# A fused attention and two-MLP kernel: two column tiles per PSUM bank, wider vector steps and finer weight loads behind the attention

## The chip, the cores and the metric

The kernel runs on one core of a Trainium2 chip. The metric is the device time of one execution in microseconds. Three executions of the kernel before took 1026.25, 1027.25 and 1030.13 us; their median is 1027.25 us. PE is the matrix engine (its weight loads are shown apart, as PEld), DVE the vector engine, ACT the scalar engine, POOL GpSimd; SP issues the DMAs.

## The reference

Block-causal attention over 4 batches, 8 heads, 576 positions of 64 elements, then two MLPs on the 2304 x 512 result. Weights arrive as float64, everything is computed to float32 accuracy.

```python
scores = scale * np.matmul(q, k.transpose(0, 1, 3, 2))
scores = np.where(block_i >= block_j, scores, -1e9)      # blocks of 64 positions
attn = softmax(scores); x = (attn @ v) -> (2304, 512)
h = x @ w1_in;  x = (h * np.cos(h)) @ w1_out             # 512 -> 2048 -> 512
h = x @ w2_in;  r = np.maximum(h, 0); out = (r * r) @ w2_out
```

## The kernel before

Every float32 operand of the MLPs is split into a high and a low part (`hi_part`, `lo_part`), and each product is three matmuls (`mm3`): high by high, high by low, low by high. Weights are read as raw 8-byte words and rebuilt as float32 (`weight_piece`), then split.

**Order.** The program is first recorded as a list of operations; `schedule` then plans them with a cost for each, as a list scheduler would: it keeps a clock for each engine and for the DMA queue, and takes the ready operation with the lowest priority number. A priority is the place in the program plus a shift by kind and phase (`PUT_OFF`). Steps that several engines can do (`flexible`: the high part on POOL or ACT, the low part on DVE or POOL, copies on ACT or DVE) go where the planned end is earliest, with each engine's cost weighted by `BIAS` of the phase. The planned order is what each engine's queue gets. Phases: 0 and 1 are the attention, 2 is stage 0, 3 is stages 1 and 2.

**Attention and the first half of MLP 1.** The attention is interleaved with the products of the first 1024 of 2048 columns of MLP 1 (`first_in`, `first_out`), whose partial result goes to DRAM (`y1_d`). In the same stretch the weights of the later stages are prepared: `left_weights` builds linear combinations of the quarters of a weight chunk (`left_parts`), splits them and stores them to DRAM (`wi_d`) by way of two buffers `so`; `staged_weights` does the like for second-product weights (`wo_d`).

**Three stages behind the attention.** Stage 0 is the second half of MLP 1 (x from `x_d`, the result to `y_d`), stages 1 and 2 are the halves of MLP 2. Each takes the 2304 tokens in four chunks of 512 and one of 256. A chunk's first product is a fast product of 2 x 2 blocks with seven multiplications: `load_quarters` loads x, forms four differences (`add`) and splits seven operands; `quad` runs the seven products for one column tile of 128 in three PSUM banks `a`, `b`, `c` of which it uses 256 columns each, with the seven weight factors as stationary operands. Between the products, finished sums are copied out (`kept`: tiles `p1`, `u2`, `p5`) or added (`summed`), and handed to `sink`, which applies the nonlinearity (`turned`: h cos h in stage 0; `squared` in stages 1 and 2) and splits the result into `g`. Each chunk has two weight chunks `c` and in each two column tiles `m`, so four calls of `quad`. The last, short chunk goes through `two`, with plain products. Then comes the second product (`out_T` in stage 0, the loop over 128-token tiles in the others), 24 matmuls for each result bank.

**Weights of the first products.** A stage's factors are loaded from `wi_d` by `factors`: for each of the two weight chunks four tiles of 1 MB, each with two factors (high and low, both halves of K). The pool `wo` has four such places, `wa` eight, four of which hold the second-product weights `w2o`. The loads for the next stage are recorded at the end of a stage (stage 0: at the last chunk), and wait for the places.

**PSUM.** Eight banks are handed out by the planner (`Banks`): up to six for `h`, up to three for `y`, and behind the attention two are kept for `y`. A bank is one unit to the planner: a step that reads any of it follows all earlier matmuls into it.

Of the kernel before, what the change touches and what calls it, by code (L numbers as in the profile page):

```python
# [24 lines left out]
BIAS = [{"DVE": 1.01, "ACT": 0.29, "POOL": 0.23}, {"DVE": 3.3, "ACT": -0.66, "POOL": -0.23}, {"DVE": 0.9, "ACT": -2.27, "POOL": -0.09}, {"DVE": -0.14, "ACT": -1.34, "POOL": 0.87}]  # L25
# [14 lines left out]
PUT_OFF = [{"load": 2, "weights": -24, "prep": 6, "scores": 25, "weighted": 31, "split": 249, "in": -31, "cos": -170, "out": -11, "warm": 9160, "later": 931}, {"load": 494, "weights": -159, "prep": -70, "scores": 69, "weighted": -175, "split": 91, "in": -32, "cos": -169, "out": -21, "later": 855}, {"load": 283, "weights": 654, "prep": -58, "scores": 43, "weighted": -284, "split": 332, "in": -36, "cos": -49, "out": -46, "later": 600}, {"in": 2, "out": 132, "later": 93}]  # L40
# [322 lines left out]
def kernel(  # L363
# [252 lines left out]
    wi_d = [[T(dram, [128, 4, 512], F32, f"wi_d{c}{i}") for i in range(4)] for c in range(6)]  # L616
    wo_d = [[T(dram, [128, 4, 512], F32, f"wo_d{c}{i}") for i in range(2)] for c in range(2)]
# [122 lines left out]
    def left_parts(w, k, slots, stage):  # L740
# [9 lines left out]
        for i, x in enumerate((a11, a12, s4, a22, s1, s2, s3, a21)):  # L750
            to = slots[i // 2][:, i % 2 * 2:i % 2 * 2 + 2, cs]
            st = T(st_p, [128, 2, 256], F32R, "so", 2) if stage else to
            hi_part(st[:, 0], x)
            lo_part(st[:, 1], x, st[:, 0])
            if stage:
                dma(to, f(st), 262144)

    @of("later")
    def left_weights(w, c, slots, stage=False):

        gate = R.ops[-1:]
        for k in range(2):
            left_parts([weight_piece(w[i * 128:i * 128 + 128, c * 512:c * 512 + 512], gate) for i in (k, k + 2)], k, slots, stage)

    def slots_of(pool, n=8, k=4):
        return [T(pool, [128, 4, 512], F32R, "w", n) for _ in range(k)]

    @of("later")
    def staged_weights(srcs, to):

        gate = R.ops[-1:]
        for src, (hi_d, lo_d) in zip(srcs, to):
            for i in range(4):
# [3 lines left out]
                dma(hi_d[:, i], f(hi), 262144)  # L777
                lo_part(lo, w, hi)
                dma(lo_d[:, i], f(lo), 262144)

    def from_dram(pool, staged, n=8):

        got = slots_of(pool, n, len(staged))
        for t, s in zip(got, staged):
            dma(f(t), s, 1048576)
        return got

    def weights(pool, srcs, n=8):

        got = []  # L790
        for src in srcs:
            hi = T(pool, [128, 4, 512], F32R, "w", n)
            lo = T(pool, [128, 4, 512], F32R, "w", n)
            for i in range(4):
                weight_part(src[i * 128:(i + 1) * 128, :], hi[:, i], lo[:, i])
# [22 lines left out]
    def h_tile(w_in, m, xs, n):  # L818
# [3 lines left out]
        for kk in range(KD):  # L822
            mm3(
                ps[:, :n], (hi[:, kk, c], lo[:, kk, c]), (xs[0][:, kk], xs[1][:, kk]),
# [20 lines left out]
    def out_T(w_out, g, n, sink):  # L845

        for d in range(KD):
            ps = bank("y")[:, :n]
            for m in range(HALF):
# [3 lines left out]
                    ps, (hi[:, m % 4, c], lo[:, m % 4, c]), (g[0][:, m, :n], g[1][:, m, :n]), m == 0, m == HALF - 1  # L853
# [307 lines left out]
    for group, steps in WORK:  # L1161
# [6 lines left out]
        if group in ((0, 2), (1, 1)):  # L1168
            c = group[0]
            left_weights(w1_in, 2 + c, wi_d[c], True)  # L1170
# [6 lines left out]
        if group == (3, 2):  # L1177
            (tmp3,) = later(("tmp3",))
            transition(s1.close, ctx, [tmp3], (xs_p, tmp))
            left = factors(wi_d[:2])  # L1180
# [4 lines left out]
    def load_plain(src, c0, n):  # L1185

        ops = [[T(x3_p, [128, 2, 256], F32R, f"x{j}{i}") for j in "hl"] for i in range(2)]
        for i in range(KD):
            t = T(x3_p, [128, 512], F32, "x", 2)[:, :n]
            dma(t, dview(src, (i, i + 1, c0, c0 + n), lambda a, i=i: a[i, :, c0:c0 + n]), n * 512)  # L1190
            hi, lo = [o[:, i % 2, :n] for o in ops[i // 2]]
            hi_part(hi, t)
            lo_part(lo, t, hi)
        return ops

    def factor(w, i, k, m):

        return [w[i // 2][:, i % 2 * 2 + j, k * 256 + m * 128:k * 256 + m * 128 + 128] for j in range(2)]

    @of("in")  # L1200
    def two(w, m, xs, n, sink):
# [9 lines left out]
    def load_quarters(src, c0, n):  # L1211

        ops = [[T(x3_p, [128, 2, 256], F32R, f"x{j}{i}") for j in "hl"] for i in range(7)]
        for k in range(2):
            raw = []
            for i in (k, k + 2):
                t = T(x3_p, [128, 512], F32, "x", 2)
                dma(t[:, :2 * n], dview(src, (i, i + 1, c0, c0 + 2 * n), lambda a, i=i: a[i, :, c0:c0 + 2 * n]), n * 1024)
                raw.append(t)
            b11, b12, b21, b22 = [t[:, o:o + n] for t in raw for o in (0, n)]  # L1220
            t1, t2, t3, t4 = [T(x3_p, [128, 256], F32, f"t{i}")[:, :n] for i in range(4)]
            add(t1, b12, b11, ALU.subtract)
            add(t2, b22, t1, ALU.subtract)
            add(t3, b22, b12, ALU.subtract)
            add(t4, b21, t2, ALU.subtract)
            for (hi, lo), x in zip(ops, (b11, b21, b22, t4, t1, t2, t3)):
                hi_part(hi[:, k, :n], x)
                lo_part(lo[:, k, :n], x, hi[:, k, :n])
        return ops

    @of("in")
    def quad(w, m, xs, n, sink):

        a, b, c = bank("h"), bank("h"), bank("h")

        def product(ps, i, first):
            hi, lo = xs[i]
            for k in range(2):
                mm3(
                    ps[:, :n], factor(w, i, k, m), (hi[:, k, :n], lo[:, k, :n]),  # L1240
                    first and k == 0, k == 1, holds=(a, b, c),
                )

        def kept(ps, tag):
            t = T(tmp3, [128, 256], F32, tag, 2)[:, :n]
            copy(t, ps[:, :n])
# [7 lines left out]
        product(a, 0, True)  # L1254
        p1 = kept(a, "p1")
        product(b, 1, True)
# [138 lines left out]
```

## Time and profile before

| | |
|---|---|
| median of three executions | 1027.25 us (1026.25 to 1030.13) |
| profiled execution | span 1029.2 us (first to last instruction); no other time is recorded with it |
| mean granted clock of PE | 0.986 |
| busy share of the span | PE 96%, PEld 84%, DVE 67%, ACT 66%, POOL 32% |
| data moved | 156.46 MB, mean 152 GB/s |

A busy share counts the time in which an instruction of the engine is shown as running. PE's matmuls overlap in the record, since the end of each is modelled; so the distance from one matmul's start to the next tells more than its duration. The granted clock is 1 at 2.4 GHz and 0.5 at 1.2 GHz; a window's value is a mean. A wait is put down to the instruction that ended last before it.

### The profile page before, as it was taken

The page shows a single profiled execution, that of the slowest core. Times are in us where ns is not written, and L with a number is a line of the kernel's source. Part 1 is how long each engine was busy: PE and PEld are TensorE (multiplying, and loading weights), DVE is VectorE, ACT ScalarE, POOL GpSimd, SP SyncE. Part 2 cuts the span into 40 slices and gives each one's busy share as a digit, 9 for nine tenths or more (in the row PEclk, how much of TensorE's full clock was granted, in tenths as well). Part 3 has the DMA queues.
Part 4 walks back from the last instruction along what each step waited for, and adds up shares of the span by engine and source line. Part 5 has one row for each costly group of instructions (what it writes and reads, how often), then busy time and mean ns, then how long its engine had stood idle before and what let it go on. Part 6 is the DMA issues. An engine that isn't in the chain of part 4 may idle for free.

```text
span 1029.2 us, 19429 instructions
## 1 busy us (share of the span) xinstructions
PE 989.5 (96%) x6672; PEld 866.6 (84%) x6672; DVE 690.6 (67%) x1813; ACT 674.4 (66%) x1781; POOL 329.4 (32%) x434
## 2 busy tenths in 40 slices
PE   7779999999999999999998998899999999999998
PEld 5657987888888889989897998788888898989986
DVE  5787686676365436386788886868868279747523
ACT  7788677888899985475585875656657365515312
POOL 4553023666787675151565520100000002000000
PEclk9889999999999999999999999999999999999999
DMA  7644232555565457612445489425465843222111
GB/s 189 179 126 124 61 93 71 161 174 145 158 181 170 129 207 272 273 44 92 128 160 180 148 290 311 177 93 184 166 203 184 294 177 116 91 82 72 63 52 61
DMA packets 137090, 156.46 MB, mean 152 GB/s; under 512 B 70688, under 2 KB 106016, under 8 KB 133408
## 3 DMA queue, kind: packets, MB, share of 16 engines
q1 hardware_dynamic: 136992, 155.23, 47.2%
q8 instruction: 52, 0.85, 0.3%
q14 instruction: 46, 0.38, 0.1%
HBM read 102.24 MB, written 52.95 MB: 151 GB/s over the span
## 4 chain that ended last, share of the span: by engine, by line
PE 72%; DMA 10%; DVE 7%; ACT 5%; POOL 2%; issue 2%; SPq 0%; ACTq 0%; DVEq 0%; POOLq 0%
PE y L529 30%; PE h L529 28%; PE t L546 5%; PE a L539 4%; DMA wi_d<-so 4%; PE s L539 3%; DMA x<-x_d 2%; DMA x<-y_d 1%; DVE r L423 1%; PE s L529 1%; DVE gl L471 1%; DMA v<-in_v_dram 1%; DVE c L430 1%; ACT c L414 1%; DMA y<-y_d 1%
## 5 line engine op out<-in xcount | busy, mean ns | idle before, releaser
L529 PE MATMUL h<-xh,w 128*128 128x256 f32 x1536 | 321.1, 285 | 7.5 <-DMA w<-wi_d 3.7
L529 PEld LDWEIGHTS h<-xh,w 128*128 128x128 f32 x1536 | 255.9, 192 | 19.9 <-ACT w L453 3.9
L529 PE MATMUL y<-gh,w 128*128 128x256 f32 (+2 forms) x832 | 213.8, 336 | 10.7 <-POOL w L448 5.0
L529 PE MATMUL h<-xl,w 128*128 128x256 f32 x768 | 216.1, 284 | 0.3 <-DVE xl L471 0.2
L529 PE MATMUL y<-w,gh 128*128 128x512 f32 x576 | 199.8, 395 | 0.9 <-ACT w L453 0.9
L529 PEld LDWEIGHTS y<-gh,w 128*128 128x128 f32 x832 | 144.9, 192 | 26.3 <-POOL w L448 6.0
L529 PEld LDWEIGHTS h<-xl,w 128*128 128x128 f32 x768 | 147.1, 192 | 3.6 <-DVE xl L471 1.0
L529 PE MATMUL y<-gl,w 128*128 128x256 f32 (+2 forms) x416 | 136.9, 333 | 1.2 <-POOL gl L467 1.2
L529 PEld LDWEIGHTS y<-w,gh 128*128 128x128 f32 x576 | 104.9, 188 | 21.2 <-ACT w L453 1.3
L529 PE MATMUL y<-w,gl 128*128 128x512 f32 x288 | 113.2, 394 | 0.0
L453 ACT ACTIVATE gh<-r 128x256 fp32r<-128x256 f32 (+1 forms) x218 | 89.1, 419 | 34.2 <-DVE r L1273 16.0
L471 DVE TENSOR_TENSOR gl<-r,gh 128x256 fp32r<-128x256 f32 (+1 forms) x168 | 79.3, 482 | 13.0 <-ACT gh L453 11.0
L944 DVE CUSTOM_DVE_ANT_0 e<-s,mask 128x384 f32<-128x384 f32 (+4 forms) x160 | 71.0, 477 | 25.0 <-PE s L539 19.8
L529 PEld LDWEIGHTS y<-gl,w 128*128 128x128 f32 x416 | 79.5, 192 | 7.7 <-POOL gl L467 2.1
L414 ACT ACTIVATE e<-e,st 128x128 f32<-128x128 f32 (+4 forms) x144 | 82.9, 579 | 4.5 <-DVE st L944 3.4
L512 POOL TENSOR_SCALAR e<-e,st 128x256 f32<-128x256 f32 (+4 forms) x105 | 65.9, 640 | 52.3 <-DVE st L965 40.3
L546 PE MATMUL t<-ident,e 128*128 128x128 f32 (+1 forms) x400 | 65.5, 283 | 3.9 <-POOL e L512 2.7
L467 POOL TENSOR_TENSOR gl<-r,gh 128x256 fp32r<-128x256 f32 (+1 forms) x64 | 54.8, 860 | 44.1 <-ACT gh L453 43.5
L423 DVE TENSOR_TENSOR o<-y,y 128x512 f32<-128x512 f32 (+1 forms) x38 | 25.0, 660 | 59.9 <-PE y L529 53.3
L482 ACT ACTIVATE r<-t 128x384 f32<-128x384 f32 (+1 forms) x108 | 55.0, 531 | 12.6 <-PE t L546 11.8
L529 PEld LDWEIGHTS y<-w,gl 128*128 128x128 f32 x288 | 54.2, 188 | 10.3 <-DVE gl L471 0.2
L423 DVE TENSOR_TENSOR r<-h,p 128x256 f32<-128x256 f32 x96 | 39.8, 417 | 32.0 <-PE h L529 31.2
(143 smaller groups left out, 1996.5 us busy)
## 6 DMA issues: line engine op xcount, KB each, us to landing
wi_d<-so SPq DMA_DIRECT2D x96, 256.0 KB, 2.7
w<-wi_d SPq DMA_DIRECT2D x24, 1024.0 KB, 7.0
raw<-in_moe_w_in_dram SPq DMA_DIRECT2D x32, 512.0 KB, 4.8
raw<-in_moe_w_out_dram SPq DMA_DIRECT2D x32, 512.0 KB, 4.0
y<-y_d SPq DMA_DIRECT2D x34, 256.0 KB, 3.0
y_d<-o SPq DMA_DIRECT2D x34, 256.0 KB, 3.4
x<-y_d SPq DMA_DIRECT2D x32, 256.0 KB, 3.1
k<-in_k_dram SPq DMA_DIRECT2D x36, 128.0 KB, 2.6
```

The lines of the kernel that those rows point to most:

```text
L414: return nc.scalar.activation(real(out), real(in_), func, **kw)
L423: out.size / 0.96 + 68, lambda: nc.vector.tensor_tensor(real(out), real(a), real(b), op=op), [out], [a, b],
L430: lambda: nc.vector.scalar_tensor_tensor(real(out), real(a), s, real(b), op0=op0, op1=op1),
L453: "ACT": ("ACT", n / 1.2 + 92, lambda: nc.scalar.activation(real(hi), real(x), ACTF.Copy)),
L467: lambda: nc.gpsimd.tensor_tensor(real(lo), real(x), real(f(hi)), op=ALU.subtract), 1,
L471: lambda: nc.vector.tensor_tensor(real(lo), real(x), real(f(hi)), op=ALU.subtract), 1,
L482: "ACT": ("ACT", n / 1.2 + 50, lambda: nc.scalar.activation(real(out), real(ps), ACTF.Copy)),
L512: lambda: nc.gpsimd.tensor_scalar(real(out), real(x), real(s), 1.0, op0=ALU.mult, op1=ALU.mult),
L529: lambda: nc.tensor.matmul(real(ps), lhsT=real(lhsT), rhs=real(rhs), start=start, stop=stop, skip_group_check=True),
L539: nc.tensor.matmul(real(ps), lhsT=real(l), rhs=real(r), start=start, stop=stop, skip_group_check=True)
L546: lambda: nc.tensor.transpose(real(out), real(in_), real(ident)[0:rows, 0:rows]), [out], [in_, ident],
L944: lambda: nc.vector.tensor_tensor_reduce(out=real(e), in0=real(ps), in1=real(m), scale=-1.0, scalar=BIG, op0=ALU.add, op1=ALU.min, accum_o ...
```

## The change

Behind the attention, `quad` and `two` are called once per weight chunk and handle both column tiles: a bank holds two tiles of 256 columns, and every vector step takes 512 columns. `load_quarters` takes two loads of 512 KB in place of four of 256 KB, and forms and splits operands over both halves of K at once. The factors are seven (the eighth, `a21`, is no longer stored; `two` uses `a21 + a22` and a difference of x in its place), each a tile of its own of 512 KB that is freed alone; `ORDERS` says which factor of the next stage takes which place, `FIRST` the order of the loads. Weights of second products are in tiles of 512 KB too, of which `wa` has 16 places. Some buffers have fewer, wider copies (`r` 4 of 256 columns to 3 of 512, `n` 2 of 256 to 1 of 512, `p1`, `u2`, `p5` 2 to 1). The planner's cost of a matmul of n columns goes from n / 2.2 to 0.4515 n + 3.5 ns, that of a transpose from 109 to 100 ns, and `BIAS` and `PUT_OFF` have new values.

```diff
-BIAS = [{"DVE": 1.01, "ACT": 0.29, "POOL": 0.23}, {"DVE": 3.3, "ACT": -0.66, "POOL": -0.23}, {"DVE": 0.9, "ACT": -2.27, "POOL": -0.09}, {"DVE": -0.14, "ACT": -1.34, "POOL": 0.87}]
+BIAS = [{"DVE": 1.84, "ACT": 0.4, "POOL": 0.23}, {"DVE": 3.3, "ACT": -0.66, "POOL": -0.23}, {"DVE": 0.9, "ACT": -3.04, "POOL": -0.02}, {"DVE": -0.14, "ACT": -3.34, "POOL": 1.15}]
-PUT_OFF = [{"load": 2, "weights": -24, "prep": 6, "scores": 25, "weighted": 31, "split": 249, "in": -31, "cos": -170, "out": -11, "warm": 9160, "later": 931}, {"load": 494, "weights": -159, "prep": -70, "scores": 69, "weighted": -175, "split": 91, "in": -32, "cos": -169, "out": -21, "later": 855}, {"load": 283, "weights": 654, "prep": -58, "scores": 43, "weighted": -284, "split": 332, "in": -36, "cos": -49, "out": -46, "later": 600}, {"in": 2, "out": 132, "later": 93}]
+PUT_OFF = [{"load": -35, "weights": -24, "prep": 14, "scores": 25, "weighted": 9, "split": 279, "in": -32, "cos": -170, "out": -10, "warm": 9160, "later": 935}, {"load": 376, "weights": -150, "prep": -70, "scores": 69, "weighted": -156, "split": 84, "in": 43, "cos": -141, "out": -21, "later": 886}, {"load": 194, "weights": 721, "prep": 429, "scores": 43, "weighted": -280, "split": 374, "in": -36, "cos": -108, "out": -53, "later": 567}, {"in": 32, "out": 14, "later": 22}]
...
-            "PE", max(109.0, passes * rhs.size / 2.2) + (108 if rhs.halves != 3 else 0),
+            "PE", max(109.0, passes * (rhs.size * 0.4515 + 3.5)) + (108 if rhs.halves != 3 else 0),
...
-            "PE", 109.0 if rows == 128 else 190.0,
+            "PE", 100.0 if rows == 128 else 190.0,
...
-    wi_d = [[T(dram, [128, 4, 512], F32, f"wi_d{c}{i}") for i in range(4)] for c in range(6)]
+    wi_d = [[T(dram, [128, 2, 512], F32, f"wi_d{c}{i}") for i in range(7)] for c in range(6)]
...
-    def factors(staged):
-        return [from_dram(*a) for a in zip((wo_p, wa_p), staged, (4, 8))]
+    ORDERS = (0, 1, 4, 3, 2, 5, 6), (4, 6, 2, 3, 0, 1, 5), (4, 0, 1, 3, 6, 2, 5)
+    def factors(staged, turn):
+        got = []
+        for pool, n, parts in zip((wo_p, wa_p), (7, 16), staged):
+            ts_ = {i: w_tile(pool, n) for i in ORDERS[turn]}
+            for i in FIRST:
+                dma(f(ts_[i]), parts[i], 524288)
+            got.append(ts_)
+        return got
+    FIRST = 0, 1, 5, 4, 6, 2, 3
+    def w_tile(pool, n=16):
+        return T(pool, [128, 2, 512], F32R, "w", n)
...
-        for i, x in enumerate((a11, a12, s4, a22, s1, s2, s3, a21)):
-            to = slots[i // 2][:, i % 2 * 2:i % 2 * 2 + 2, cs]
-            st = T(st_p, [128, 2, 256], F32R, "so", 2) if stage else to
+        for t, x in zip(to, (a11, a12, s4, a22, s1, s2, s3)):
+            st = T(st_p, [128, 2, 256], F32R, "so", 2)
             hi_part(st[:, 0], x)
             lo_part(st[:, 1], x, st[:, 0])
...
+    def raw_rows(src, c0, n):
+        raw = []
+        for i in (0, 2):
+            t = T(x3_p, [128, 2, 512], F32, "x", 2)[:, :, :n]
+            dma(t, dview(src, (i, i + 2, c0, c0 + n), lambda a, i=i: a[i:i + 2, :, c0:c0 + n].rearrange("k p c -> p k c")), n * 1024)
+            raw.append(t)
+        return raw
...
+    def product(ps, w, i, x, first, holds=()):
+        hi, lo = x
+        for m in range(2):
+            for k in range(2):
+                c = slice(k * 256 + m * 128, k * 256 + m * 128 + 128)
+                mm3(ps[:, m], (w[i][:, 0, c], w[i][:, 1, c]), (hi[:, k], lo[:, k]), first and not m + k, k == 1, holds)
...
-        for i, left in enumerate(((0, 1), (7, 3))):
-            ps = bank("h")
+        for i, left in enumerate(((0, 1), (4, 3))):
+            ps = h_bank()
             for j in range(2):
-                hi, lo = xs[j]
-                for k in range(2):
-                    mm3(ps[:, :n], factor(w, left[j], k, m), (hi[:, k, :n], lo[:, k, :n]), not j + k, j + k == 2)
-            sink(i, 0, ps[:, :n])
+                product(ps, w, left[j], xs[j * (i + 1)], not j)
+            sink(i, 0, ps)
...
-            t = T(tmp3, [128, 256], F32, "r", 4)[:, :n]
-            tt(t, ps[:, :n], x, ALU.add)
+            t = T(tmp3, [128, 2, 256], F32, "r", 3)
+            tt(t, ps, x, ALU.add)
...
-        t = T(tmp3, [128, 256], I32, "n", 2)[:, :n]
+        t = T(tmp3, [128, 2, 256], I32, "n", 1)
...
-                for m in range(2):
-                    def sink(i, j, h, m=c * 4 + m, n=n, g=g, stage=stage):
-                        r = (squared if stage else turned)(h, n)
-                        hi, lo = [x[:, m + 2 * i, j * n:j * n + n] for x in g]
+                def sink(i, j, h, c=c, g=g, stage=stage):
+                    r = (squared if stage else turned)(h)
+                    m = c * 4 + 2 * i
+                    hi, lo = [x[:, m:m + 2, j * 256:j * 256 + 256] for x in g]
```

## Rows read from the trace of the kernel before

**Rows 1.** The page's head and busy times: us (share of span) xinstructions.

```profile
span 1029.2 us, 19429 instructions
PE 989.5 (96%) x6672; PEld 866.6 (84%) x6672; DVE 690.6 (67%) x1813; ACT 674.4 (66%) x1781; POOL 329.4 (32%) x434
```

**Rows 2.** Windows: busy us (xcount) by engine, granted clock, DMA share, GB/s.

```profile
0.00:100.00 100.00, 80.21 (x531) 60.52 (x532) 74.99 (x201) 78.13 (x194) 49.31 (x70) 0.91 0.57 154
...
400.00:420.00 20.00, 18.87 (x112) 17.72 (x111) 11.50 (x23) 12.40 (x30) 11.91 (x14) 0.91 0.71 270
540.00:560.00 20.00, 16.53 (x76) 13.34 (x75) 17.57 (x32) 13.12 (x34) 13.95 (x17) 0.91 0.39 120
620.00:640.00 20.00, 18.74 (x149) 17.82 (x148) 13.03 (x37) 8.34 (x25) 0.00 (x0) 1.00 0.95 313
640.00:660.00 20.00, 16.28 (x105) 15.26 (x104) 17.03 (x42) 15.01 (x37) 0.77 (x2) 0.91 0.63 223
```

**Rows 3.** Chain that ended last, in order of time: start us, us, what.

```profile
427.01 18.12 PE h L529 x150
...
532.18 3.88 DMA wi_d<-so
...
613.67 12.22 DMA wi_d<-so
...
639.77 5.32 DMA w<-wi_d
...
1014.06 11.32 PE y L529 x48
```

**Rows 4.** Groups by line and form from 380 us on, PE's matmuls.

```profile
L529 PE MATMUL h<-xh,w 128*128 128x256 f32 x1536 | 321.1, 285 | 7.5 <-DMA w<-wi_d 3.7 <-ACT p L482 2.0 <-DVE r L423 1.1
L529 PE MATMUL y<-w,gh 128*128 128x512 f32 x576 | 199.8, 395 | 0.9 <-ACT w L453 0.9
L529 PE MATMUL y<-gh,w 128*128 128x512 f32 x256 | 82.3, 398 | 3.3 <-ACT gh L453 3.3
```

**Rows 5.** Waits from 380 us on: us in total, times, longest.

```profile
PE y L529 <- ACT gh L453: 3.3, 1, 3.3
...
PE y L529 <- POOL gl L467: 1.2, 3, 0.5
...
ACT so L453 <- DMA wi_d<-so: 19.7, 16, 5.1
```

**Rows 6.** Groups by form from 380 us on, DVE and ACT, both widths.

```profile
L471 DVE TENSOR_TENSOR gl<-r,gh 128x256 fp32r<-128x256 f32 x152 | 69.6, 468 | 11.4 <-ACT gh L453 10.4
L453 ACT ACTIVATE gh<-r 128x256 fp32r<-128x256 f32 x174 | 69.4, 412 | 25.6 <-DVE r L1273 16.0 <-DVE r L423 5.5 <-PE y L529 3.1
L423 DVE TENSOR_TENSOR r<-h,p 128x256 f32<-128x256 f32 x96 | 39.8, 417 | 32.0 <-PE h L529 31.2 <-ACT s L414 0.5
L482 ACT ACTIVATE p<-h 128x256 f32<-128x256 f32 x93 | 34.6, 379 | 34.2 <-PE h L529 33.8
L423 DVE TENSOR_TENSOR o<-y,y 128x512 f32<-128x512 f32 x34 | 23.3, 688 | 55.4 <-PE y L529 52.7 <-DMA y<-y_d 2.7
L471 DVE TENSOR_TENSOR w<-c,w 128x512 fp32r<-128x512 f32 x16 | 11.5, 721 | 1.0 <-ACT w L453 1.0
L482 ACT ACTIVATE o<-y 128x512 f32<-128x512 f32 x18 | 10.5, 591 | 16.8 <-PE y L529 15.1 <-DMA y_d<-o 1.7
L453 ACT ACTIVATE w<-c 128x512 fp32r<-128x512 f32 x16 | 10.0, 627 | 8.3 <-DVE c L430 6.9 <-PE y L529 1.4
```

**Rows 7.** DMA issues: out<-in, queue, operation, xcount, KB each, us to landing.

```profile
wi_d<-so SPq DMA_DIRECT2D x96, 256.0 KB, 2.7
```

**Rows 8.** PE's waits before 380 us.

```profile
PE t L546 <- DMA k<-in_k_dram: 7.0, 3, 4.7
PE y L529 <- POOL w L448: 5.0, 3, 3.5
```

More of the change, by code (lines that the diff above doesn't have):

```diff
@@ L771, in staged_weights @@
         gate = R.ops[-1:]
-        for src, (hi_d, lo_d) in zip(srcs, to):
+        for src, pairs in zip(srcs, to):
             for i in range(4):
@@ L776, in staged_weights, with rows_of, from_dram, weights @@
                 hi_part(hi, w)
-                dma(hi_d[:, i], f(hi), 262144)
+                dma(pairs[i // 2][0][:, i % 2], f(hi), 262144)
                 lo_part(lo, w, hi)
[L779 to L788, printed above, removed]
+                dma(pairs[i // 2][1][:, i % 2], f(lo), 262144)
+    def rows_of(pairs):
+        return [[t[:, i] for pair in pairs for t in pair[j:j + 1] for i in range(2)] for j in range(2)]
+    def from_dram(staged):
+        got = [[w_tile(wa_p) for _ in range(2)] for _ in staged]
+        for pair, src in zip(got, staged):
+            for t, d in zip(pair, src):
+                dma(f(t), d, 524288)
+        return rows_of(got)
+    def weights(pool, srcs):
         got = []
         for src in srcs:
-            hi = T(pool, [128, 4, 512], F32R, "w", n)
-            lo = T(pool, [128, 4, 512], F32R, "w", n)
+            pairs = [[w_tile(pool) for _ in range(2)] for _ in range(2)]
+            hi, lo = rows_of(pairs)
             for i in range(4):
-                weight_part(src[i * 128:(i + 1) * 128, :], hi[:, i], lo[:, i])
+                weight_part(src[i * 128:(i + 1) * 128, :], hi[i], lo[i])
             got.append((hi, lo))
@@ L1169 @@
             c = group[0]
[L1170 removed]
+            left_weights(w1_in, 2 + c, wi_d[c])
         if group in ((1, 2), (2, 1)):
@@ L1179 @@
             transition(s1.close, ctx, [tmp3], (xs_p, tmp))
-            left = factors(wi_d[:2])
+            left = factors(wi_d[:2], 0)
         first_out(*group, g)
[L1185 to L1193, printed above, removed]
-        return ops
@@ L1196, in factor, with x_parts @@
-    def factor(w, i, k, m):
-        return [w[i // 2][:, i % 2 * 2 + j, k * 256 + m * 128:k * 256 + m * 128 + 128] for j in range(2)]
+    def raw_rows(src, c0, n):
[5 more added lines that the diff above has]
+        return raw
+    def x_parts(forms):
+        ops = []
+        for j, x in forms:
+            hi, lo = [T(x3_p, [128, 2, 256], F32R, f"x{i}{j}") for i in "hl"]
+            hi_part(hi, x)
+            lo_part(lo, x, hi)
+            ops.append((hi, lo))
+        return ops
@@ new lines, in load_plain, with load_quarters @@
+    def load_plain(src, c0):
+        x1, x2 = raw_rows(src, c0, 256)
+        d = T(x3_p, [128, 2, 256], F32, "t0")
+        add(d, x2, x1, ALU.subtract)
+        return x_parts(((0, x1), (1, x2), (4, d)))
+    def load_quarters(src, c0):
+        raw = raw_rows(src, c0, 512)
+        b11, b12, b21, b22 = [t[:, :, o:o + 256] for t in raw for o in (0, 256)]
+        t1, t2, t3, t4 = [T(x3_p, [128, 2, 256], F32, f"t{i}") for i in range(4)]
+        add(t1, b12, b11, ALU.subtract)
+        add(t2, b22, t1, ALU.subtract)
+        add(t3, b22, b12, ALU.subtract)
+        add(t4, b21, t2, ALU.subtract)
+        return x_parts(enumerate((b11, b21, b22, t4, t1, t2, t3)))
@@ L1231, in quad, with times_ @@
-    @of("in")
[L1232 to L1242, printed above, removed]
+                product(ps, w, left[j], xs[j * (i + 1)], not j)
+            sink(i, 0, ps)
+    @of("in")
+    def quad(w, xs, sink):
+        a, b, c = h_bank(), h_bank(), h_bank()
+        def times_(ps, i, first):
+            product(ps, w, i, xs[i], first, (a, b, c))
@@ L1294, in squared @@
     @of("cos")
-    def squared(h, n):
+    def squared(h):
         if not psum(h):
@@ L1307 @@
         if stage == 2:
-            left = factors(wi_d[4:])
+            left = factors(wi_d[4:], 2)
         for i in range(5):
@@ L1327 @@
                 else:
-                    w2o = [from_dram(wa_p, c) for c in wo_d]
+                    w2o = [from_dram(c) for c in wo_d]
             if stage < 2 and 0 < i < 3:
                 c = 2 * stage + i - 1
-                left_weights(w2_in, c, wi_d[2 + c], True)
+                left_weights(w2_in, c, wi_d[2 + c])
             if stage == 0 and i == 4:
-                left = factors(wi_d[2:4])
+                left = factors(wi_d[2:4], 1)
             if stage == 0:
```

77 lines of the change are left out of this document (29 added, 48 removed).

## The prediction

> **What bounds the kernel now.** I read the page's head first: PE is busy 96% of the span, the vector engines (DVE, ACT) two thirds, POOL a third [rows 1]. Busy shares are averages, so next come the windows [rows 2]. They part the run in two. Up to 380 us attention runs: PE stands still for 20 us of the first 100. After 380 us, in the part that the change rewrites, PE is busy in nearly every window.
>
> A busy PE need not be at its peak, so I work out what the matmuls of this part cost at their best. A run of 150 matmuls of 256 columns takes 18.12 us in the chain, of which the last one's own 0.28 us is only drained once: (18.12 - 0.28)/149 = 119.7 ns each. The last 48 of 512 columns take (11.32 - 0.39)/47 = 232.5 ns each [rows 3]. The three stages hold 2304 of the former in the first products (the 1536 with the high part and half as many with the low part), 1248 of 512 columns in the second products (576 + 288 and 256 + 128) and 192 of 256 columns for the short chunk [rows 4]. That is 275.8 + 290.2 + 23.0 = 589.0 us. What the first MLP's first half leaves behind 380 us, by the code 192 matmuls of 320 columns and some 31 of 256, adds by the same rate per column 32.4 us: 621.4 us. The last matmul ends at 1014.06 + 11.32 = 1025.38 us, 645.4 us after 380. So PE loses **24.0 us** here, and that is the ceiling of what a change of the vector steps and weight loads can win while the matmuls stay as they are.
>
> Where the 24 us lie: PE's waits name 3.7 us for a weight load, 3.3 us for a high part of g (`gh`), 2.0 + 1.1 us for the kept and summed products (`p`, `r`), 0.9 us for a converted weight and 1.2 us for a low part of g [rows 4, 5]: 12.2 us. In three 20 us windows the granted clock reads 0.91 [rows 2]: 0.09 x 20 = 1.8 us each, 5.4 us. Each of them holds a stop of PE just before it. 6.4 us are short gaps with no name. The Trainium skill (TensorE: Matmul & The Clock Gate, "Why this matters for your kernels") says that a pause of matmuls sends the clock from 2.4 to 1.2 GHz. The rows agree, and by the rule as by them a stop that goes takes its 1.8 us with it.
>
> **The change part by part.** *Matmuls.* `quad` ran once per column tile with 42 matmuls; now once per chunk half with 84. The products, their 256 columns and the 128-column weights are the same: 0.
>
> *Vector steps.* Every step between `h` and `g`, and the splitting of x, goes from two instructions of 256 columns to one of 512. By rows of both widths [rows 6], DVE's subtract for the low part falls from 2 x 468 to 721 ns, its adds out of PSUM from 2 x 417 to 688, ACT's high part from 2 x 412 to 627, its copies out of PSUM from 2 x 379 to 591: 23, 17, 24 and 22% less. Behind 380 us eleven groups of DVE are widened (the largest 69.6 us, together 379 us) and ten of ACT (the largest 69.4 us, together 298 us) [rows 6]; a fifth of them is some 80 us of DVE and 60 us of ACT. None of it is time by itself, since PE is the bound. It counts at three places.
>
> (a) The stop at 540 us. The chain there goes over ACT, which holds a staging step (`so`) until a store to `wi_d` has landed (3.88 us), and then over a string of DVE and ACT steps that were late; PE waits 3.3 us for `gh` and then runs at the lower clock: 3.3 + 1.8 = 5.1 us. In that window DVE is busy 17.6 of 20 us [rows 2, 3, 5]. With a fifth less vector work the backlog should be gone before PE needs it; the staging itself stays, 14 stores a weight chunk for 16. Between 0 and 5.1 I take **-4**, nearer the upper end because the backlog, not the landing, is the longer piece of the chain.
>
> (b) The short waits for `p` and `r`, 3.1 us. The second use of a bank comes one product after the first: 6 x 119.7 = 0.72 us of cover before, 12 x 119.7 = 1.44 us now, while the copy only grows from 0.38 to 0.59 us. Between 0 and 3.1: **-3**.
>
> (c) The short nameless gaps: **-1.5** of the 6.4, for the same reason; bounds 0 and 4.
>
> *Weight factors.* A stage loads 14 pieces of 512 KB in place of 8 of 1 MB, 7 MB for 8, and a piece can start as soon as its own factor is free. Before, a slot holds two factors, and three of four slots of a half are still in use by the short last chunk (`two` reads factors 0, 1, 7, 3); now `two` reads 0, 1, 4, 3, so 2, 5 and 6 come free one product group earlier, and the orders written in `ORDERS` give their places to the factors that are needed first. What this can win is the stop at 640 us: 3.7 us of waiting for `w<-wi_d`, and 1.8 us of clock. The chain ahead of it is a queue of transfers: stores to `wi_d`, one of which lands after 12.2 us, then the load, 5.3 us, in windows where the DMA engines are 95% busy [rows 2 to 4]. An eighth less traffic and an earlier start speak for the whole 5.5, the full DMA engines for nothing: I take **-4.5**; bounds 0 and 5.5.
>
> *DMA issues on SP.* Stores to `wi_d` go from 96 to 84 [rows 7]; by the code, loads of factors from 24 to 42, of x from 60 to 30, of `wo_d` from 4 to 8: 184 become 164. Nothing is gained by that, as SP's queue is not in the stops above other than through landing times: 0.
>
> *What is later.* A PSUM bank is one tile to the scheduler, so no step reads a column tile before the other one's six matmuls are done. At the end of a chunk half `g` comes later by 0.72 us and by the wider steps of the chain: for the squared stages (591 - 379) + (688 - 418) + (627 - 414) + (721 - 441) ns = 0.98 us [rows 6], together **1.7 us**. What hides it is the next chunk's `quad`, 10 us of matmuls ready to run, and the second products of the six rows of g (of eight) that are done. At the last chunk, 48 second-product matmuls run at the end, and only a quarter of them need the last rows. I take 0; the bounds are 0 and 1.7 us at each of 15 chunks. The Trainium skill (PSUM, "PSUM bank collisions raise a hardware error") says that an engine may not read a bank in which TensorE writes, even at other columns. No row shows a collision, but the rule rules out an early read of the first half and so speaks against two tiles in a bank.
>
> *Attention.* Four of 32 staging pairs fall away (the eighth factor), and priorities and the planner's bias move. No matmul changes. PE's named waits before 380 us are led by loads of k (7.0 us) and by POOL's weight parts (5.0 us) [rows 8]. The new bias of the first phase makes DVE look dearer, which can push more onto POOL or out of DVE's queue. I see no sign and take 0, with 10 us either way as bounds, half of PE's 20 idle us of the first 100.
>
> **Sum.** -4 - 3 - 1.5 - 4.5 = -13. The profiled execution spans 1029.2 us, 2 us above the median of 1027.25 and inside the spread of the runs; no other time stands beside its span. Set against the median: 1027.25 - 13 = **1014 us**, -1.3%. For this kernel about 0.5% (5.1 us, below 1022 or above 1032.4) can be told from no change.
>
> **The rivals.**
> (1) *All stops go and attention gains too.* 24.0 us is the ceiling behind 380 us; with most of it and a few us of attention, 1003. For it: vector engines with a fifth less work. Against: some waits (the end of the first MLP's cosines at 410 us, 1.2 + 1.8; weights converted at 665 us) lie in code that is not touched.
> (2) *The transfers stay the bound at 530 and 640 us*, and the change does not do what it says there: -4 and -4.5 do not come, 1027.25 - 4.5 = 1023. For it: 95% busy DMA engines, and ACT's 19.7 us of waiting for `wi_d` stores [rows 5], a wait that is kept. Against: less traffic, finer pieces.
> (3) *The new priorities cost attention* some 10 us by POOL's weight parts: 1024. Against: the small shifts in that phase.
> (4) *Slower: the later `g`.* If the second products wait at each chunk's end, 1.7 us a chunk and 15 chunks are 25.4 us: 1014 + 25 = 1039. It decides (above 1032.4) from 11 of 15 chunks on, or fewer if a stop long enough for the clock to fall comes with it: 1.7 + 1.8 us needs 6. For it: the planner fills both queues with bigger blocks: a quad holds three banks for 84 matmuls where it held them for 42. Against: PE waits for `gh` once in three stages [rows 5], since other work lies between.
>
> **How the numbers follow.** Forecast 0.46 (own range 1008 to 1021); rival 1 0.15; rival 2 0.18; rival 3 0.08; rival 4 0.13. Faster: 0.46 + 0.15 + about two fifths of rival 2 and a quarter of rival 3 = 0.70. Slower: rival 4 and a little of rival 3 = 0.14. The same: the rest, 0.16. The range must leave out no more than 0.2: below 1001 lies about 0.06 (rival 1 with a large gain in attention), above 1031 about 0.14 (rival 4), so 1001 to 1031.
>
> **What would show it.** Right: from 380 us to PE's last matmul some 632 us instead of 645; one or no window at 0.91 instead of three; DVE's and ACT's busy time behind 380 us lower by about 80 and 60 us with no like gain in time; the waits for `p` and `r` gone; the wait for `w<-wi_d` under 1 us. Wrong: a wait of PE for `gh` or `gl` at the chunks' ends (rival 4), windows of full DMA with PE waiting for `w<-wi_d` (rival 2), or a shift of attention's end by more than 5 us (rivals 1 and 3).

## The result and the profile after

The changed kernel takes 1040.34 us (1038.25 to 1042.44) against 1026.86 for the one before: ratio 1.0113, 95% interval 1.0076 to 1.015. It is slower by 1.1%, where 1.3% faster was forecast. The profiled execution took 1038.25 us and spans 1036.5, so the two traces show 7.3 us of the difference of 13.5.

The page's head and busy times of the changed kernel, beside [rows 1]:

```profile
span 1036.5 us, 18463 instructions
PE 990.8 (96%) x6672; PEld 863.7 (83%) x6672; DVE 641.0 (62%) x1344; ACT 636.4 (61%) x1417; POOL 340.6 (33%) x412
```

DVE and ACT are 50 and 38 us less busy, and yet the time is longer, since PE's 6672 matmuls set it. Its last matmul ends at 1024.47 + 8.28 = 1032.75 us in the chain, 652.8 us after 380; before it was 645.4, forecast was 632. The windows (columns as in [rows 2]) show where PE stands:

```profile
0.00:380.00 380.00, 357.08 (x2701) 294.64 (x2702) 219.65 (x712) 320.63 (x837) 231.47 (x325) 0.98 0.49 140
...
580.00:600.00 20.00, 16.14 (x100) 14.05 (x98) 12.97 (x16) 12.98 (x25) 15.76 (x14) 1.00 0.60 178
600.00:620.00 20.00, 18.55 (x85) 15.74 (x86) 17.47 (x26) 8.79 (x17) 3.99 (x4) 0.91 0.91 314
640.00:660.00 20.00, 20.00 (x157) 19.46 (x157) 20.00 (x34) 17.63 (x32) 1.39 (x1) 1.00 0.38 118
...
780.00:800.00 20.00, 17.25 (x94) 14.82 (x95) 17.72 (x32) 11.26 (x23) 0.00 (x0) 0.91 0.48 162
```

By 380 us PE has issued 2701 matmuls, much the same as before (2707 in that window of the kernel before), so in this pair of traces the loss lies behind the attention. The stop at 640 us is gone, and of the one at 540 us little is left (PE is busy for 18.5 of the 20 us there, at a clock of 1.00). New ones stand near 590 and 790 us, each with a fall of the clock. PE's waits from 380 us on:

```profile
PE y L529 <- ACT gh L453: 10.9, 7, 3.1
PE y L529 <- POOL gl L467: 2.9, 3, 2.2
PE h L529 <- ACT p L482: 2.8, 4, 1.3
PE h L529 <- ACT u L482: 1.3, 3, 0.9
PE h L529 <- DVE r L423: 0.8, 1, 0.8
```

The wait for a factor is gone; that for the high part of g went from 3.3 us, once [rows 5], to 10.9 us, seven times. The chain shows what is ahead of it at both stops:

```profile
584.84 5.75 DMA x<-y_d
...
595.03 1.15 DVE r L423
596.17 1.15 DVE s L430
...
785.00 5.96 DMA x<-y_d
...
791.04 0.63 ACT xh L453
791.67 0.53 ACT gh L453
...
796.04 4.14 PE y L529 x10
```

Near 790 us a load of x lands 5.96 us after its issue. ACT, whose queue is in order, stands first 2.9 us for a store to `wi_d` and then 2.1 us for this load, with a split of x (`xh`); `gh`, for which PE waits, stands behind. The stop near 590 us has the same head (a load of x, 5.75 us) and then DVE steps of 1.15 us each.

### The profile page after: what moved, and what is told of

Its sections match the earlier page's. It is cut to its first block, busy times and chain, and to the rows that moved or that the text cites. A ratio compares the mean times of both kernels' runs of the same rounds, so it can differ in the third digit from the quotient of the medians.

```text
span 1036.5 us, 18463 instructions
## 1 busy us (share of the span) xinstructions
PE 990.8 (96%) x6672; PEld 863.7 (83%) x6672; DVE 641.0 (62%) x1344; ACT 636.4 (61%) x1417; POOL 340.6 (33%) x412
## 4 chain that ended last, share of the span: by engine, by line
PE 54%; DMA 15%; ACT 10%; POOL 8%; DVE 8%; issue 4%; SPq 0%; POOLq 0%; ACTq 0%; DVEq 0%
PE y L529 24%; PE h L529 18%; PE t L546 5%; DMA wi_d<-so 5%; PE a L539 4%; DMA x<-y_d 3%; PE s L539 2%; POOL xl L467 2%; DMA raw<-in_moe_w_in_dram 2%; DMA w<-wi_d 2%; POOL e L512 2%; ACT gh L453 2%; DMA x<-x_d 2%; DVE r L423 1%; ACT e L414 1%
## 5 line engine op out<-in xcount | busy, mean ns | idle before, releaser
L529 PE MATMUL h<-xh,w 128*128 128x256 f32 x1536 | 289.8, 284 | 5.0 <-ACT p L482 2.8
L529 PEld LDWEIGHTS h<-xh,w 128*128 128x128 f32 x1536 | 244.5, 192 | 9.1 <-ACT p L482 3.8
L529 PE MATMUL y<-w,gh 128*128 128x512 f32 x576 | 185.0, 398 | 2.6 <-ACT gh L453 2.6
L529 PEld LDWEIGHTS y<-w,gh 128*128 128x128 f32 x576 | 107.9, 189 | 29.1 <-ACT gh L453 4.2
L453 ACT ACTIVATE gh<-r 128x512 fp32r<-128x512 f32 (+2 forms) x134 | 74.4, 558 | 67.2 <-DVE r L1291 32.5
L512 POOL TENSOR_SCALAR e<-e,st 128x384 f32<-128x384 f32 (+4 forms) x134 | 83.4, 637 | 44.1 <-DVE st L977 31.7
L471 DVE TENSOR_TENSOR gl<-r,gh 128x512 fp32r<-128x512 f32 (+2 forms) x88 | 65.8, 752 | 15.0 <-ACT gh L453 11.8
L467 POOL TENSOR_TENSOR gl<-r,gh 128x256 fp32r<-128x256 f32 (+2 forms) x60 | 56.2, 938 | 37.9 <-ACT gh L453 37.2
L482 ACT ACTIVATE p<-h 128x512 f32<-128x512 f32 x48 | 28.3, 589 | 64.2 <-PE h L529 64.2
```

Source lines behind the costliest of these rows:

```text
L453: "ACT": ("ACT", n / 1.2 + 92, lambda: nc.scalar.activation(real(hi), real(x), ACTF.Copy)),
L467: lambda: nc.gpsimd.tensor_tensor(real(lo), real(x), real(f(hi)), op=ALU.subtract), 1,
L471: lambda: nc.vector.tensor_tensor(real(lo), real(x), real(f(hi)), op=ALU.subtract), 1,
L482: "ACT": ("ACT", n / 1.2 + 50, lambda: nc.scalar.activation(real(out), real(ps), ACTF.Copy)),
L512: lambda: nc.gpsimd.tensor_scalar(real(out), real(x), real(s), 1.0, op0=ALU.mult, op1=ALU.mult),
L529: lambda: nc.tensor.matmul(real(ps), lhsT=real(lhsT), rhs=real(rhs), start=start, stop=stop, skip_group_check=True),
```

## The experiments

Each ratio is to runs of the kernel before on the same chip, with its 95% interval. Stated times in us differ from chip to chip, so ratios are compared.

| run | structure | plan | ratio |
|---|---|---|---|
| e1 | new | old | 0.9924 (0.9901 to 0.9946) |
| e2 | old | new | 1.0136 (1.0095 to 1.0177) |
| e3 | seven factors alone | old | 0.9950 (0.9926 to 0.9973) |
| e4 | new | new, one shift 567 to 571 | 1.0118 (1.0074 to 1.0162) |
| e5 | new | new, but old behind the attention | 1.0015 (0.9998 to 1.0031) |
| e6 | new | new, but old in the attention | 1.0121 (1.0101 to 1.0141) |
| e7 | new | old, new costs of PE | 1.0035 (1.0002 to 1.0067) |
| e8 | new | old, no subtract on POOL late | 0.9825 (0.9809 to 0.9842) |
| e9 | new | new, no subtract on POOL late | 0.9971 (0.9948 to 0.9995) |
| e10 | old | old, no subtract on POOL late | 0.9934 (0.9906 to 0.9962) |
| e11 | new | old, one shift 600 to 590 | 0.9935 (0.9908 to 0.9963) |
| e12 | new | e7 and no subtract on POOL late | 0.9924 (0.9896 to 0.9951) |
| e13 | new | old, new cost of a transpose | 1.0048 (1.003 to 1.0065) |
| e14 | new | old, new cost of a matmul | 1.0053 (1.0031 to 1.0074) |
| e15 | new | new, old bias behind the attention | 1.0093 (1.006 to 1.0126) |
| e16 | new | new, old shifts behind the attention | 0.9998 (0.9975 to 1.0021) |
| e17 | new | new, old shifts in stages 1 and 2 | 1.0005 (0.9987 to 1.0023) |
| e18 | new | new, x's loads planned longer | 0.9998 (0.9978 to 1.0018) |

### Structure or plan (e1 to e4)

"Plan" is what leaves the work as it is and moves only its order and the engine that takes a flexible step: `BIAS`, `PUT_OFF` and PE's planned costs. e1 and e2 swap these lines between the two kernels, whole:

```diff
-BIAS = [{"DVE": 1.84, "ACT": 0.4, "POOL": 0.23}, ...
+BIAS = [{"DVE": 1.01, "ACT": 0.29, "POOL": 0.23}, ...
...
-            "PE", max(109.0, passes * (rhs.size * 0.4515 + 3.5)) + (108 if rhs.halves != 3 else 0),
+            "PE", max(109.0, passes * rhs.size / 2.2) + (108 if rhs.halves != 3 else 0),
```

> The changed kernel with the bias, the priority shifts and PE's planned costs of the kernel before: the new structure alone. Theory V (512-column steps are longer blocks in the in-order queues of ACT, DVE and POOL, so the high part of g comes late): no nearer to before than the changed kernel, 1036 to 1046 us, with PE's waits for gh and gl near 14 us behind 380 us. Rival P (the new priorities are at fault): 1015 to 1028 us, waits for gh under 5 us.

> The kernel before with the new bias, priority shifts and planned costs of PE: the new priorities alone. Theory V: within 8 us of before, 1020 to 1035 us, no p or gh wait over 2 us more than before. Rival P: 1036 us or more, with PE's waits for gh behind 380 us near 10 us.

e3 puts the seven tiles, their orders and the factors that `two` uses after the change into the kernel before, with a difference of x in 256-column steps:

```diff
-        for i, left in enumerate(((0, 1), (7, 3))):
+        for i, left in enumerate(((0, 1), (4, 3))):
...
-                hi, lo = xs[j]
+                hi, lo = xs[j * (i + 1)]
...
+            d = T(x3_p, [128, 256], F32, "t1")[:, :n]
+            add(d, raw[1], raw[0], ALU.subtract)
```

> The kernel before with seven factors in tiles of 512 KB that are freed one by one, 256-column steps and the old priorities: the weight part alone. Both theories: the wait for a factor at the end of the first stage (3.7 us and 1.8 us of clock) goes, 1019 to 1025 us. If the weight part is at fault: 1032 us or more.

e4 moves one number:

```diff
-"out": -53, "later": 567}
+"out": -53, "later": 571}
```

> The changed kernel with one priority shift of the first stage moved by 4 places (staged weights, 567 to 571): how far the time moves with an order that is different for no reason. Theory V: 1034 to 1046 us, since every order has the long blocks. Rival P (a bad order): it can fall by more than 8 us, below 1032 us.

Theory V, the first I held, falls: the new structure is 0.8% faster with the old plan, and the old structure 1.4% slower with the new one (there with 5.1 us of waits for `gh`, not the 10 of rival P). The weight part alone brings 0.5% (5.1 us). That leaves 0.3% for the wide steps if the two add, but the intervals of e1 and e3 overlap, so this rest is not told from nothing. An order that is different for no reason (e4) leaves the loss where it is. Windows and PE's waits of e1:

```profile
0.00:380.00 380.00, 358.68 (x2730) 298.80 (x2731) 243.13 (x763) 315.85 (x832) 210.15 (x295) 0.98 0.49 140
```

```profile
PE y L529 <- ACT gh L453: 7.2, 7, 1.6
PE y L529 <- POOL gl L467: 1.3, 3, 0.5
```

`gh` is waited for seven times here too (rival P said under 5 us in all), but never for longer than 1.6 us, and between 580 us and the end of the matmuls the clock falls once (0.98 and 0.94 in the windows from 600 and 620 us) where it falls twice in the changed kernel. PE's last matmul ends 634.4 us after 380, against the 632 forecast and the 652.8 of the changed kernel.

### Which part of the plan, and POOL (e5 to e8)

e5 and e6 put the old entries of `BIAS` and `PUT_OFF` back for two of the four phases and keep the new planned costs; e7 is e1 with the new planned costs. e8 is e1 with

```diff
-        R.any([alts[e] for e in FREE[kind].split()[:1 if kind == "wt" and R.phase < 2 else 9]], w, r)
+        names = "DVE" if kind in ("lo", "add") and R.phase > 1 else FREE[kind]
+        R.any([alts[e] for e in names.split()[:1 if kind == "wt" and R.phase < 2 else 9]], w, r)
```

> The changed kernel with the old bias and priority shifts of the stages behind the attention (phases 2 and 3) alone; those of the attention and PE's planned costs stay new. Theory S (the new shifts behind the attention are at fault: the first run's trace, without them, loses 15 us of PE behind 380 us where the changed kernel loses 30): 0 to 7 us below before, waits for gh behind 380 us under 8 us. Rival A (the shifts of the attention are at fault, by what they leave late at its end): 6 us or more above before.

> The counterpart: the old bias and shifts of the attention (phases 0 and 1) alone, the stages behind it keep the new ones. Theory S: 5 to 12 us above before, PE's waits for gh behind 380 us near 11 us. Rival A: 3 us or more below before.

> The changed structure with the old bias and shifts, and PE's new planned costs (matmul 0.4515 n + 3.5 ns, transpose 100 ns) in place of the old ones. Theories S and A: within 4 us of the same kernel with the old costs, so 4 to 12 us below before. Rival C (the new costs spoil the order): above before.

> The new structure with the whole old plan, and behind the attention no subtract or difference on POOL: low parts and differences go to DVE alone. Theory Q (POOL's 512-column subtracts, 1.6 us each against 0.7 on DVE, and DVE's steps of 1.15 us beside them make g late): DVE's steps fall to 0.69 us, waits for gh and gl under 5 us, 3 to 8 us below the same kernel with POOL. Rival D (DVE fills up): PE waits more for DVE's steps, at or above the same kernel with POOL.

The loss has two parts. The shifts or bias behind the attention account for 1.0% (the changed kernel against e5), and the new planned costs for 1.1% (e7 against e1); the new shifts of the attention change little in the time (e6 against the changed kernel, e5 against e7). e5 comes to 1.5 us above before, where theory S said below. More than half of the costs' part lies in the attention: the same window of e7 shows 60 matmuls fewer by 380 us than e1's 2730, at 0.13 us each some 8 us:

```profile
0.00:380.00 380.00, 358.63 (x2670) 295.50 (x2671) 238.40 (x756) 311.47 (x818) 204.00 (x289) 0.97 0.48 137
```

One trace is a rough measure of this: e3, e8 and e11, whose vector engines have the same order up to 390 us as e1's, show 2711, 2703 and 2706 matmuls in that window. Read from the starts of PE's matmuls, the 2700th starts at 376.4 to 379.6 us in these four, at 383.4 to 386.3 us with the new costs and the old shifts (e6, e7, e12), and at 379.8 to 382.7 us in the changed kernel and the seven others with its order in the attention (e4, e5, e9, e15 to e18). So the new costs alone cost some 6 us there, of the 11 us of their 1.1%, and the new shifts of the attention win about half of the 6 back.

For e7 I expected wrong under theories S and A, and rival C holds beside S.

e8 is the fastest kernel of the study, 1.75% below before. Groups by form behind 380 us, first of the changed kernel, then of e8:

```profile
L471 DVE TENSOR_TENSOR gl<-r,gh 128x512 fp32r<-128x512 f32 x76 | 58.7, 778 | 11.9 <-ACT gh L453 10.8
L430 DVE SCALAR_TENSOR_TENSOR s<-n,r 128x512 f32<-128x512 int32 x36 | 36.9, 1024 | 3.8 <-ACT n L414 3.6
L423 DVE TENSOR_TENSOR r<-h,p 128x512 f32<-128x512 f32 x48 | 32.9, 686 | 41.5 <-PE h L529 41.2 <-ACT xh L453 0.2
L467 POOL TENSOR_TENSOR xl<-x,xh 128x512 fp32r<-128x512 f32 x10 | 17.0, 1705 | 47.1 <-ACT xh L453 47.1
```

```profile
L472 DVE TENSOR_TENSOR gl<-r,gh 128x512 fp32r<-128x512 f32 x84 | 58.3, 706 | 3.9 <-ACT gh L454 3.6
L430 DVE SCALAR_TENSOR_TENSOR s<-n,r 128x512 f32<-128x512 int32 x36 | 24.6, 684 | 2.3 <-ACT n L414 2.1
L423 DVE TENSOR_TENSOR r<-h,p 128x512 f32<-128x512 f32 x48 | 33.0, 687 | 43.7 <-PE h L530 41.6 <-ACT gh L454 1.5 <-ACT xh L454 0.4
```

Over this stretch, steps with both inputs in SBUF last 1024 and 778 ns on the mean with POOL's subtracts beside some of them, 684 and 706 without; the add out of PSUM is 686 or 687 ns either way. The Trainium skill (SBUF — State Buffer, "Who interferes with whom") says that a DVE instruction with two SBUF inputs contends with a GpSimd instruction that reads SBUF, and one with at most one SBUF input does not. The rows agree on both. POOL's own subtract of 512 columns lasts 1.6 to 1.7 us, so its steps are slow themselves, and e8 does not part the two. In e8 PE's last matmul ends 625.4 us after 380, 4 us above the 621.4 us of the prediction. The gain over e1, 1.0%, is more than theory Q's 3 to 8 us.

### Is it POOL, or the order (e9 to e12)

e9, e10 and e12 make e8's edit in the changed kernel, in the kernel before and in e7; e11 is e1 with the shift of staged weights in the first stage at 590 instead of 600.

> The changed kernel, whole new plan, with no subtract or difference on POOL behind the attention. Theory Q (the new plan is slow because it puts POOL's long subtracts, and DVE's steps slowed beside them, where g is due): most of the loss goes, 10 to 18 us below before, DVE's 512-column steps at 0.69 us, waits for gh behind 380 us under 5 us. Rival R (the order itself is bad: x's loads and steps stand ahead of g's on ACT and DVE): no more than 8 us below the changed kernel, so 1028 us or more where before is 1027, and waits for gh over 7 us.

> The kernel before (256-column steps, old plan) with no subtract or difference on POOL behind the attention. If POOL's share alone is the matter, wide steps or not: 10 us or more below before. If DVE has room for it only with 512-column steps (it stands at 88% of a window before): between 4 below and 10 above before.

> The new structure with the old plan and one shift of the first stage moved from 600 to 590 (staged weights), which changes the order of all engines. If the old plan's gain on the new structure is luck of one order: at before or above it. If the order's details matter little: within 3 us of the same kernel without it, 5 to 11 us below before.

> The new structure with the old bias and shifts, no subtract or difference on POOL behind the attention, and PE's new planned costs. Theory Q: the new costs cost less than 4 us now, since what they spoil is where POOL's steps stand: 14 to 19 us below before. Rival R: they cost the same 1% as with POOL, 5 to 9 us below before.

Taking POOL's subtracts away wins 1.0, 1.4, 0.7 and 1.1% with the four, so it is a gain of its own, in the old structure too. It does not carry off the plan's loss: e9 is 1.5% above e8 (1.9% for the changed kernel against e1), e12 is 1.0% above e8. So theory Q falls as the cause of the slowdown. Rival R is right for e12 and for the waits for `gh` in e9 (7.4 us, of which POOL made 3.4 us at one stop), but e9 is 1.4% below the changed kernel, more than the rival's 8 us, since POOL's share is a gain beside the order. The stop near 790 us stays in e9 (2.3 us for `gh`, clock 0.91), with no subtract on POOL. e10 gains 0.7%, between its two forecasts. e11 shows that the old plan's gain on the new structure does not hang on one order.

### The two parts taken apart (e13 to e16)

e13 and e14 are e1 with one of the two new costs, e15 and e16 the changed kernel with the old `BIAS` or the old `PUT_OFF` in phases 2 and 3.

> The new structure with the old plan but a transpose's planned cost of 100 ns instead of 109 (the trace shows 109 ns from one to the next). If the transposes' cost is what the new costs lose by, the time is 5 to 12 us above the same kernel with 109, and PE has done some 40 matmuls fewer by 380 us. Otherwise within 3 us of it.

> The new structure with the old plan but matmuls planned at 0.4515 n + 3.5 ns instead of n / 2.2. If this is what the new costs lose by, 5 to 12 us above the same kernel with the old costs, PE some 40 matmuls behind at 380 us. Otherwise within 3 us of it.

> The changed kernel with the old bias behind the attention, its shifts new. If the bias (ACT's cost counted still more negative) is at fault: 7 to 11 us below the changed kernel, PE's waits for gh under 8 us. If the shifts are: within 4 us of the changed kernel.

> The changed kernel with the old priority shifts behind the attention, its bias new. If the shifts (cosine steps 108 places early instead of 49, second products of the last stages 14 late instead of 132) are at fault: 7 to 11 us below the changed kernel, waits for gh under 8 us and the stop of PE at a chunk's end near 790 us gone. If the bias is: within 4 us of the changed kernel.

Behind the attention it is the shifts: with the old ones the loss of 1.1% is gone, with the old bias 0.9% stay. But PE still waits 9.0 us for `gh` in e16, where under 8 was forecast, so shorter waits for `gh` are not all that the old shifts bring. Of the planned costs either alone loses as much as both together (1.2 and 1.3%), though one is a number further from the trace (a transpose follows the next after 109 ns) and the other nearer to it (0.4515 x 256 + 3.5 = 119.1 ns, measured 119.7). So it is no matter of the better number. PE's last matmul ends 13.7 and 13.5 us later than in e1. By 380 us PE has issued 2616 and 2685 matmuls where e1 has 2730 (some 40 fewer were forecast): with the transpose's cost the loss is nearly all in the attention (114 x 0.13 = 15 us, 11 against the lowest of e3, e8 and e11), with the matmul's cost no more than 6 us of it are, and the rest is behind. What in the attention's old order is better was not tried further and stays open.

### The stop near 790 us (e17, e18)

e17 is the changed kernel with the old `PUT_OFF` of phase 3; e18 leaves every shift and tells the planner how long x's loads are:

```diff
-            dma(t, dview(src, (i, i + 2, c0, c0 + n), lambda a, i=i: a[i:i + 2, :, c0:c0 + n].rearrange("k p c -> p k c")), n * 1024)
+            dma(t, dview(src, (i, i + 2, c0, c0 + n), lambda a, i=i: a[i:i + 2, :, c0:c0 + n].rearrange("k p c -> p k c")), n * 1024, n * 1024 / 140)
```

> The changed kernel with the old shifts of the last two stages alone (second products 132 late instead of 14); the first stage keeps the new ones. If the stop near 794 us comes from these: it is gone, and the time is 4 to 7 us below the changed kernel, PE losing some 24 us behind 380 us instead of 30. If the first stage's shifts make it: within 2 us of the changed kernel, stop kept.

> The changed kernel, all shifts new, with x's loads of 512 KB planned to take 3.7 us of the DMA queue instead of 1.2, so that they land as late in the plan as they do in the trace (5.5 us after issue). If a step of x that is planned too early and holds ACT is the mechanism: the stops near 590 and 794 us go, 6 to 11 us below the changed kernel. If not: within 4 us of it, with stops for gh elsewhere.

Both come back to the time of before, 1.1% below the changed kernel (11 us for e17, where 4 to 7 were forecast). In e18 both stops are gone with no shift changed. ACT's waits for loads of x, first of the changed kernel, then of e18, and e18's windows:

```profile
ACT xh L453 <- DMA x<-y_d: 8.0, 2, 5.9
ACT xh L453 <- DMA x<-x_d: 3.6, 1, 3.6
```

```profile
ACT xh L453 <- DMA x<-x_d: 1.2, 1, 1.2
```

```profile
580.00:600.00 20.00, 19.12 (x116) 16.44 (x117) 19.87 (x20) 16.58 (x31) 16.95 (x15) 1.00 0.44 146
780.00:800.00 20.00, 20.00 (x112) 17.35 (x111) 15.75 (x28) 11.10 (x21) 0.00 (x0) 1.00 0.56 188
```

So what makes the two stops is borne out: with the new shifts, steps of x are placed where the plan believes their loads have landed (1.75 us and 1.2 us of service after issue, by the code), these two loads take 5.75 and 5.96 us, and ACT's queue holds `gh` behind them. e18 does not change ACT's order alone: in its plan the transfers behind a load of x land later too. The load is planned to land 5.5 us after its issue; the two loads land after 4.7 and 4.5 us in its trace. e17 puts the stop at 790 us on the shifts of the last two stages, but not by way of the load: ACT waits 1.5 and 1.6 us for x there in e16 and e17 too, and PE has other matmuls to run meanwhile. The stop near 590 us stays in e17 (2.4 us for `gl`, 2.3 us for `gh`), though its ratio is that of e16.

The stops are not all of the late 1%. With the old shifts of the last stages, PE's queue alternates between second products (512 columns) and first products (256); here in e16:

```profile
792.08 0.28 PE L529 MATMUL h<-xh,w 128*128 128x256 f32 x1
792.20 0.39 PE L529 MATMUL y<-w,gh 128*128 128x512 f32 x1
792.42 0.28 PE L529 MATMUL h<-xl,w 128*128 128x256 f32 x1
```

Behind 430 us a 512-column matmul follows one of 256 columns 652 times in e16, 103 times in the changed kernel and 105 times in e18. Where PE does not wait, the next start in e16 comes on the mean 116.4 ns after a 256-column matmul if one of 512 follows and 119.6 ns if another of 256 does, and 230.3 ns after one of 512 if one of 256 follows, 231.8 ns if not. Counted against the prediction's 119.7 and 232.5 ns, that saves e16 and e17 some 4 us over the three stages and the changed kernel nothing. This is an estimate from the starts in the traces, as no run changes the alternation alone. PE's last matmul ends 10.5 us earlier in e16 than in the changed kernel, so this is about two fifths of it. e18 has the same ratio without it. How the late 1% divides between the stops and the alternation is therefore not settled: the profiled executions of e16, e17 and e18 span 1026.0, 1031.2 and 1028.5 us, while their ratios agree.

## Why the prediction was wrong

The step that failed is the sum, -4 - 3 - 1.5 - 4.5: it has no term for the new plan behind the attention. The prediction speaks of the plan only in "*Attention.* ... I see no sign and take 0". I costed what each instruction does and took the order for neutral. It was not: with the new structure the new plan costs 1.9% (the changed kernel against e1), and PE's last matmul comes 18.4 us later. PE's new planned costs make 1.1% of it (e7 against e1) and the new shifts behind the attention 1.0% (e5) to 1.1% (e16); the new shifts of the attention give a little back.

Most of it is not in the attention: there the changed kernel's order costs some 3 us (the 2700th matmul, above), inside the 10 us of bounds, and the sign of rival 3, an end of the attention shifted by more than 5 us, did not come. Behind 380 us PE loses some 31 us where the forecast left 24 - 13 = 11; with the old plan (e1) it loses 16. These two allow for the matmuls left at 380 us in each trace.

Rival 4's time, 1039 us, is near the measured 1040, and its sign, PE waiting for `gh` at the chunks' ends, came. The number is luck: e1 has the same two tiles in a bank and the same wide steps, and is 0.8% faster than before.

Point by point:
- *Matmuls 0*: the same matmuls, but their spacing hangs on the order. A 512-column one follows one of 256 columns 480 times before, 650 times in e1 and 103 times in the changed kernel; against the kernel before that is, by the estimate above, some 2 us won in e1 and 2 us lost in the changed kernel. *SP's issues 0*: nothing in the runs speaks against it.
- *Weight factors -4.5*: right. e3 alone is 5.1 us below before (2.8 to 7.6), and the wait for `w<-wi_d` is in no list of PE's waits of the changed kernel.
- *Vector steps -4, -3, -1.5*: too large by threefold. e1 less e3 is 0.26%, 2.7 us, with overlapping intervals. The stop at 540 us did shrink (PE busy 18.4 of 20 us in e1 and 18.5 in the changed kernel, 16.5 before, and no fall of the clock). The waits for `p` and `r` are 3.1 us before, 1.0 us in e1 and 3.6 us in the changed kernel: that term came in part, and not with the new plan. Some of what was won was taken back by the next point.
- *What is later: 0*: wrong in e1 already. PE waits for `gh` 7.2 us, seven times, where it waited 3.3 us once. That is rival 4's mechanism at about a sixth of its price (3.9 of 25.4 us). The long stops of the changed kernel came where ACT was held by a load.
- *DVE and ACT 80 and 60 us less busy behind 380 us*: 25 and 41 us (421.4 for 446.9, 315.8 for 357.1). The rows of 512 columns that I took read PSUM or came from stretches where POOL was mostly quiet, and I did not ask why DVE's steps of 256 columns on `s` and `r` lasted 542 and 601 ns before; without POOL's subtracts (e10) they last 427 and 419. In the changed kernel the wide steps on `s` and `r` last 1.0 us on the mean, and POOL's own wide step (1.57 to 1.7 us) saves about a tenth over two narrow ones (0.86 to 0.91 each), not a fifth.
- *The ceiling of 24 us behind 380 us*: no run passes it, and the best, e8, reaches 20. But it is no strict ceiling, since alternating matmuls (632 times in e8) take some 4 us less than the 119.7 and 232.5 ns that it is worked out from.
- *The total of the structure, -13*: measured -0.76%, 7.8 us; with the plan's +1.9% the changed kernel lands at +1.1%.

## What to carry to other kernels

In a kernel whose order is planned from costs and shifts, new costs and shifts are a part of the change with a price of their own: swap them between the two kernels first, as that one pair of runs says more than any sum over instructions. Where engines' queues are in order, ask of every step that waits for a load what stands behind it, and plan loads by the landing that the trace shows under load. Count what an order does to the bound engine itself, here the matmuls that follow each other, and not only its waits. Before work is moved to an engine because it is idle, look at how long its steps take there and what they do to the engine beside it: keeping POOL's subtracts off the last stages makes the best kernel here, 0.9825 of before with the new structure and the old plan.

## What the runs showed of the hardware

DVE's 512-column steps on two SBUF inputs run in step with POOL's 256-column ones in the changed kernel near 596 us: one starts every 1.15 us on either engine; with POOL quiet DVE's last 0.69 us. Loads of x of 512 KB from `y_d` take 3.9 us from issue to landing in the median, but 5.75 and 5.96 us at the two stops. ACT's 512-column high part of `r` is 628 ns in the changed kernel and 627 ns in e8, without POOL's subtracts. At a granted clock of 1 the next matmul starts 116.4 ns after one of 256 columns if it has 512 columns, 119.6 ns if it has 256 (e16, means).
